# A layer norm, linear attention and gated MLP block on one core: the order of the first eleven microseconds

## The chip, the cores and the metric

The kernel runs on one core of a Trainium2 chip. The metric is the device time of one execution in microseconds (us); lower is better.

## The reference

One sequence of 2048 tokens with 448 features. The input is normalised once; a linear attention with 16 heads of 28 and an MLP with 1792 hidden units both read the normalised input, and the MLP's output gates the attention's. All inputs are bf16.

```python
x  = A_x                                   # (1, 2048, 448)
xn = (x - mean(x)) / sqrt(var(x) + 1e-5)   # over the 448 features

q, k, v = split(xn @ wqkv)                 # (448, 3*448), 16 heads of 28
phi = lambda t: where(t > 0, t + 1, exp(t)) + 1e-6
kv  = einsum("bhsd,bhse->bhde", phi(k), v)
z   = einsum("bhsd->bhd", phi(k))
o   = einsum(phi(q), kv) / (einsum(phi(q), z) + 1e-6)
s   = o @ wo

h = relu(xn @ w1 + b1) ** 2                # (448, 1792)
g = silu(h @ w2 + b2)                      # (1792, 448)
out = x + s * g
```

## The kernel before

**Tiles.** The 2048 tokens are 16 tiles of 128, in four groups of four. The 448 features are contracted in three full chunks of 128 rows and a rest of 64. In `xn` the last 64 columns are copied once more beside themselves (the "twin", L529), so that a transposed rest fills 128 rows and two matmuls with 64 rows each can stand side by side in the array. The 1792 hidden units are 14 blocks of 128; `H g.f` is block f of token group g.

**Who orders the work.** The function builds a list of operations with `add`, each with an engine, an estimated duration, what it reads and writes, and in some cases other engines that could take it (`alts`). `schedule` then plays the list through a model in time. TensorE ("pe") and SP keep the order in which the code names their operations. ScalarE ("act"), VectorE ("dve") and GpSimd ("pool") are planned greedily: among the operations that are ready, the one with the smallest due time `late` goes first, and `prio` sets that due time by hand. Transfers are modelled with one shared stream that is free from `dma_free` on (L118). The plan fixes each engine's order, the engine of operations with alternatives, and the PSUM bank of each buffer. `emit` writes the order out with semaphore waits; on the chip each engine then runs its list in that order, and a waiting instruction holds everything behind it on its engine.

**Transfers of the head.** SP issues them one after another: x tile 0, x tile 1, x tiles 2 and 3 in one transfer (`load_x`, L450 to L452), the first 384 rows of w_k (`load_main`, L453), then w1 in three blocks of columns, with the boundaries in `cuts` (L449: 512, 768 and 512 columns), each as 384 rows and two rests of 32 to 96 KB each (`load_rest`); b1 goes behind the first block, x tiles 4 to 7 behind the second. The two rests of w_k and the first rest of the first w1 block are issued from ScalarE. A matmul of block f waits for all transfers of the w1 block in which it lies (L770); blocks 0 and 1 (`HA = 2`) are the "head" blocks and are treated apart.

**The first group, tiles 0 to 3.** Per tile (L1211): `bn` and `ag` are statistics on VectorE (L483, L484), `ln` and `rs` give the reciprocal deviation on ScalarE (L491, L495), `xn` is the norm on VectorE (L513). `pe_transpose` turns the three full chunks on TensorE (L590) and copies them out of PSUM on ScalarE or VectorE (L600, L599): in its call `((0, 3, "act"),)` names chunks 0 to 3 and the engine of the copy. `pe_transpose_rests` does the rest chunk of two tiles (L614, copy on ScalarE L624). `k_part` are k's matmuls for one tile (L788), `k_rests` the 64-row rest of two tiles (L803), followed by the feature map phi (exp on ScalarE, two steps on VectorE). `head_part(lo, fi)` are the full chunks of w1 block fi for tiles lo and lo+1 (L816), `head_rest` their 64-row rest for all four tiles (L832). `warm(n)` emits n matmuls on a tile of zeros, whose result nobody reads (L1206); `warm(9, [("mv", 0)])` also waits for the statistics of tile 0. `bias_cols` turns b1 into columns (L1221).

TensorE runs this in the order in which it stands from L1226 on. Behind it come, at L1331, blocks 2 to 13 of group 0 in pairs (L773): first the pair of blocks 2 and 3, then, eight matmuls later, blocks 4 and 5, and so on. The rest of the kernel (q, k, the MLP's second matmul L1079, the attention's sums, the gate) follows on TensorE in a fixed order as well.

Of the kernel before, what the change touches and what calls it, by code (L numbers as in the profile page):

```python
# [9 lines left out]
P = 128  # L10
S, D, F = 2048, 448, 1792
# [35 lines left out]
class Program:  # L47
# [5 lines left out]

    def add(self, eng, emit, reads=(), writes=(), dur=0.2, alts=(), nbytes=0, mode=None, label="", slow=1.0):
        op = Op(eng, emit, reads, writes, dur, alts, nbytes, mode, label)
        op.slow = slow
        for t in op.reads:
            op.raw.add(self.writer[t])
            self.readers.setdefault(t, []).append(op)
        for t in op.writes:  # L60
            w = self.writer.get(t)
            if w is not None and w is not op:
                op.deps.add(w)
            for r in self.readers.get(t, ()):
                if r is not op:
                    op.deps.add(r)
            self.writer[t] = op
            self.readers[t] = [r for r in self.readers.get(t, ()) if r is op]
        op.raw.discard(op)
        op.deps |= op.raw  # L70
        for d in op.deps:
            d.succ.append(op)
        self.ops.append(op)
        return op
# [23 lines left out]
    def one_pass(self):  # L98
# [16 lines left out]
                        users[b].append(op)  # L115
        bank_last = [None] * PSUM_BANKS
        free = dict.fromkeys(self.ENGINES, 0.8)
        dma_free = 2.3  # L118
        last_mode = None
        order = {e: [] for e in self.ENGINES}  # L120
        pend = {e: [] for e in self.ENGINES}
# [4 lines left out]

        def ready(op):
            r = 0.0
            for d in op.deps:
                if d.end is None:  # L130
                    return None
                same = d.eng == op.eng == "pe" and d is not op.sync
                r = max(r, d.end + (0.0 if same else 0.05 if d.nbytes else LAT[d.eng]))
            return r
# [14 lines left out]
        while n:  # L149
            best = None  # L150
            for e in self.ENGINES:
                if e in fixed:
                    if not pend[e]:
                        continue
                    op = pend[e][0]
                    r = ready(op)
                    if r is None:
                        continue
                    new = [b for b in op.writes if isinstance(b, Buf) and b.bank is None]
                    banks = []  # L160
                    if new:
# [4 lines left out]
                        r = max(r, times[len(new) - 1][0])  # L166
                    st = max(r, free[e] + (SWITCH if e == "pe" and last_mode not in (None, op.mode) else 0.0))
                    cand = (st, 0, op, e, banks, op.dur)
                else:
# [13 lines left out]
                    for op in pend[e]:  # L183
                        r = ready(op)
                        if r is not None:
                            cands.append((max(r, free[e]), op))
                    for o in floating:
                        if o.end is None:
                            for ae, _ in o.alts:
                                if ae == e and o.eng != e:  # L190
                                    r = ready(o)
# [3 lines left out]
                    for st, op in cands:  # L195
                        if op.alts:
                            mine = op.dur if op.eng == e else dict(op.alts)[e]
                            others = [(op.eng, op.dur)] + list(op.alts)
                            r = ready(op)
# [7 lines left out]
                    if not keep:  # L207
                        continue
                    m = min(keep, key=lambda k: k[0])
                    st, op, du = min(  # L210
                        (k for k in keep if k[0] <= m[0] + min(0.6 * m[2], 0.02 + max(0.0, 0.3 * (m[1].late - k[1].late)))),
                        key=lambda k: k[1].late,
                    )
# [3 lines left out]
            st, _, op, e, banks, du = best  # L217
# [8 lines left out]
            if op.nbytes:  # L226
                free[e] = st + op.dur
                s2 = max(dma_free, st + 1.0)
                dma_free = s2 + op.nbytes * op.slow / (280e3 if s2 < 13.0 else 330e3)
# [76 lines left out]
def bass_recurrent_scan__linear_attn_block__dense_activation_squared_relu__prompt_kernel(  # L306
    nc, A_x, A_wqkv, A_wo, B_x, B_w1, B_b1, B_w2, B_b2, out
):
    with ExitStack() as es:
        sb = lambda name, shape, dtype: es.enter_context(nc.sbuf_tensor(name, shape, dtype))  # L310
        bf, f32 = dt.bfloat16, dt.float32
        pr = Program()
# [14 lines left out]
        w_k = sb("w_k", [P, 4, D], bf)  # L327
# [10 lines left out]
        mv = sb("mv", [P, NT, 2], f32)  # L338
# [79 lines left out]
        def tiles(t, lo, hi):  # L418
            if hi <= 2:
                return t[0][P * lo : P * hi].rearrange("(p s) d -> p s d", s=1)  # L420
            base, n = (2, 2) if hi <= 4 else (lo // 4 * 4, 4)
            v = t[0][P * base : P * (base + n)].rearrange("(p s) d -> p s d", s=n)
            return v[:, lo - base : hi - base, :]

        def dma(eng, dst, src, writes, nbytes, reads=(), dur=0.45, slow=1.0):
            return add(
                eng, lambda e, _: e.dma_start(dst, src), reads, writes, dur, nbytes=nbytes, label="dma" + str(writes[0]), slow=slow
            )

        def load_x(lo, hi, eng="sp"):  # L430
            dma(eng, x_tok[:, lo:hi, :], tiles(A_x, lo, hi), [("x", i) for i in range(lo, hi)], (hi - lo) * P * D * 2)

        def load_main(eng, w, src, name, lo, hi, c0=0, c1=3, off=0):
            dma(
                eng, w[:, c0:c1, lo:hi],
                src[128 * c0 : 128 * c1, off + lo : off + hi].rearrange("(c p) j -> p c j", p=P),
                [(name, c) for c in range(c0, c1)], 128 * (c1 - c0) * (hi - lo) * 2,
            )

        def load_rest(eng, w, src, name, lo, hi, off=0):  # L440
            for i in (0, 1):
                dma(
                    eng if isinstance(eng, str) else eng[i], w[64 * i : 64 * i + 64, 3, lo:hi], src[384:448, off + lo : off + hi], [(name, 3 + i)],
                    64 * (hi - lo) * 2, dur=0.58,
                )

        wn = lambda name: [(name, i) for i in range(5)]
        HA = 2
        cuts = (0, 4 * P, 10 * P, F)  # L449
        load_x(0, 1)  # L450
        load_x(1, 2)
        load_x(2, 4)  # L452
        load_main("sp", w_k, A_wqkv, "wk", 0, D, off=D)  # L453
        load_rest("act", w_k, A_wqkv, "wk", 0, D, off=D)
        for n, (lo, hi) in enumerate(zip(cuts, cuts[1:])):
            load_main("sp", w_1, B_w1, f"w1{n}", lo, hi)
# [125 lines left out]
        def pe_transpose(si, pieces):  # L582
            for lo, hi, eng in pieces:
                b = Buf("T")

                def f(e, _, lo=lo, hi=hi, b=b):
                    v = ps(b)[:, :].bitcast(bf)
                    last = None
                    for c in range(lo, hi):
                        last = e.transpose(v[:, (c - lo) * P : (c - lo + 1) * P], xn[:, si, c * P : (c + 1) * P], ident[:, :])  # L590
                    return last

                add("pe", f, [("xn", si), "ident"], [b], 0.0558 * (hi - lo), mode="128", label=f"T{si}.{lo}")

                def ev(e, eng, lo=lo, hi=hi, b=b):
                    src = ps(b)[:, 0 : 64 * (hi - lo)].bitcast(bf)
                    dst = xT[:, si, lo:hi, :].rearrange("p c k -> p (c k)")
                    if eng == "dve":
                        return e.tensor_copy(dst, src)  # L599
                    return e.activation(out=dst, in_=src, func=AF.Copy)  # L600

                n = hi - lo
                add(
                    eng, ev, [b], [("xT", si, c) for c in range(lo, hi)],
                    0.15 + 0.07 * n if eng == "dve" else 0.18 + 0.107 * n, label=f"eT{si}.{lo}",
                ).prio = -30
# [178 lines left out]
        def k_part(si, lo, hi):  # L785
            def f(e, _):
                for c in range(lo, hi):
                    last = e.matmul(  # L788
                        ps(k_head[si])[:, 0:D], xT[:, si, c, :], w_k[:, c, :], start=(c == 0), stop=False, skip_group_check=True
                    )  # L790
                return last

            add(
                "pe", f, [("wk", c) for c in range(lo, hi)] + [("xT", si, c) for c in range(lo, hi)] + ([k_head[si]] if lo else []),
                [k_head[si]], (hi - lo) * MM(D), mode="128", label=f"K{si}.{lo}",
            )
# [30 lines left out]
        def head_rest(lo):  # L827
            fs = (lo, lo + 1)

            def f(e, _):  # L830
                for h, fi in enumerate(fs):
                    last = e.matmul(  # L832
                        ps(head[fi])[:, 0:512], w_1[half[h], 3, fi * P : (fi + 1) * P], xT[half[h], 0:4, 3, :], start=False,
                        stop=True, skip_group_check=True,
                    )
                return last

            bs = [head[fi] for fi in fs]
            add("pe", f, [("xT", i) for i in range(4)] + [("w10", 3), ("w10", 4)] + bs, bs, MM(512), mode="64", label=f"Hr{lo}")
            for fi in fs:  # L840
                h_out(head[fi], 0, fi)
# [358 lines left out]
        def warm(n, after=()):  # L1200
            b = Buf("W")

            def f(e, _):
                last = None
                for _i in range(n):
                    last = e.matmul(ps(b)[:, 0:P], dum[:, 0:P], dum[:, 0:P], start=True, stop=True)  # L1206
                return last

            add("pe", f, ["dum", *after], [b], n * 0.075, mode="128", label="warm")
# [13 lines left out]
            )  # L1223
            add("act", lambda e, _: e.activation(out=b1f[:, :], in_=ps(bb)[:, 0 : NF // 2].bitcast(bf), func=AF.Copy), [bb], ["b1f"], 0.2, label="b1f")

        warm(31)  # L1226
        warm(9, [("mv", 0)])
        pe_transpose(0, ((0, 3, "act"),))
        warm(7)
        pe_transpose(1, ((0, 3, "dve"),))  # L1230
        k_part(0, 0, 3)
        pe_transpose_rests(0)
        k_part(1, 0, 3)
        head_part(0, 0)
        pe_transpose(2, ((0, 3, "dve"),))
        head_part(0, 1)
        k_rests(0)
        warm(4)
        pe_transpose(3, ((0, 3, "dve"),))
        bias_cols()  # L1240
        pe_transpose_rests(2)
        warm(4)
        head_part(2, 0)
        head_part(2, 1)
        head_rest(0)

        def ln(lo, hi):
            for si in range(lo, hi):
# [91 lines left out]
        a, b = "G10|G11", "G12|G13"  # L1340
# [37 lines left out]
```

## Time and profile before

| | |
|---|---|
| runs | 144.44, 144.80, 144.85 us; median 144.8 |
| the profiled execution | 144.75 us; span from first to last instruction 143.0 us |
| granted TensorE clock | 1.00 |
| TensorE matmul busy | 139.0 us (97% of the span), 1310 matmuls |
| VectorE busy | 104.3 us (73%) |
| ScalarE busy | 77.2 us (54%) |
| GpSimd busy | 6.4 us (4%) |
| chain that ended last | 96% on TensorE |
| HBM read, written | 9.23 MB, 1.90 MB |

TensorE counts as busy with any matmul, the fillers of L1206 among them. "L773" is line 773 of the kernel; a row of the timeline gives the start, the time from the first start to the last end of the merged instructions, the engine, the operation, what it writes and reads, and in brackets how long the engine was idle before and what ended that. A row of the chain gives the start, how long the chain ran through this engine and line, and how many instructions that were. A row of transfers gives the issuing queue, how many, KB of each and the median us from issue to landing. Starts and lengths are in us.

### The profile page before, as it was taken

To read this page: it belongs to the slowest core of one execution; us is meant where nothing else is said; L and a number is where in the kernel's file an instruction comes from. 1 tells how busy PE (TensorE), PEld (TensorE's weight loads), DVE (VectorE), ACT (ScalarE), POOL (GpSimd) and SP (SyncE) were. 2 spreads that over 40 slices of the span, in tenths; PEclk is the share of its full clock that TensorE was granted. 3 is DMA by queue.
4 is the path that set the end of the run, shared out by engine and by line. 5 is a ranking of instruction groups with operands and counts; after the bars stand their busy time and mean duration, and the time that the engine had idled before them with its cause. 6 is when DMAs were issued, how large, how long until landed. Compare 5 with 4: busy or idle time off the path is not lost.

```text
span 143.0 us, 3268 instructions
## 1 busy us (share of the span) xinstructions
PE 139.0 (97%) x1310; PEld 72.2 (50%) x1310; DVE 104.3 (73%) x226; ACT 77.2 (54%) x142; POOL 6.4 (4%) x40
## 2 busy tenths in 40 slices
PE   7999999999999999999999999999999999999991
PEld 7964445554444444444544444435546455555471
DVE  2779998997398899769787799782035727865874
ACT  3566996030788724997862787698139430202311
POOL 7900000000000000000000000000000000000000
PEclk9999999999999999999999999999999999999999
DMA  4999995259732000223000000000687001223032
GB/s 110 305 300 306 322 306 91 38 141 291 86 49 37 5 0 0 46 43 54 9 5 0 0 0 5 0 0 18 171 197 152 3 5 34 94 64 101 32 126 67
DMA packets 23500, 12.91 MB, mean 90 GB/s; under 512 B 14274, under 2 KB 22718, under 8 KB 23486
## 3 DMA queue, kind: packets, MB, share of 16 engines
q1 hardware_dynamic: 21758, 11.40, 31.2%
q10 hardware_dynamic: 1728, 1.31, 4.2%
q8 instruction: 10, 0.16, 0.5%
q14 instruction: 4, 0.03, 0.1%
HBM read 9.23 MB, written 1.90 MB: 78 GB/s over the span
## 4 chain that ended last, share of the span: by engine, by line
PE 96%; DVE 2%; issue 0%
PE pb L773 29%; PE pb L1079 22%; PE pb L1171 7%; PE pb L874 7%; PE pb L716 6%; PE pb L726 6%; PE pb L1206 4%; PE pb L1096 4%; PE pb L1136 3%; PE pb L853 1%; DVE gbuf L1160 1%; PE pb L880 1%; PE pb L816 1%; PE pb L1023 1%; PE pb L788 1%; PE pb L590 1%
## 5 line engine op out<-in xcount | busy, mean ns | idle before, releaser
L773 PE MATMUL pb<-xT,w 64*128 64x512 bf16 x378 | 43.6, 376 | 0.0
L1079 PE MATMUL pb<-w,r 64*128 64x448 bf16 x336 | 34.1, 349 | 0.0
L751 ACT ACTIVATE r<-pb,b1f 128x512 bf16<-128x512 f32 x40 | 25.9, 687 | 14.2 <-PE pb L773 13.4
L773 PEld LDWEIGHTS pb<-xT,w 64*128 64x128 bf16 x378 | 18.4, 94 | 21.7
L1079 PEld LDWEIGHTS pb<-w,r 64*128 64x128 bf16 x336 | 16.3, 94 | 15.8 <-issue 0.4
L748 DVE TENSOR_SCALAR r<-pb,b1f 128x512 bf16<-128x512 f32 x16 | 11.7, 748 | 5.5 <-PE pb L773 5.3
L763 ACT ACTIVATE r<-r 128x1024 bf16<-128x1024 bf16 x14 | 14.6, 1061 | 0.5 <-DVE r L748 0.4
L1191 DVE TENSOR_TENSOR gbuf<-pb,gbuf 128x448 bf16<-128x448 f32 x14 | 8.1, 619 | 6.1 <-PE pb L1171 6.1
L483 DVE BATCH_NORM_STATS2 st<-x_tok 128x6 f32<-128x448 bf16 x16 | 9.4, 616 | 3.1 <-DMA x_tok<-in_A_x_dram 2.9
L716 PE MATMUL pb<-w_k,xT 64*128 64x448 bf16 x98 | 11.6, 349 | 0.0
L1069 DVE TENSOR_TENSOR gbuf<-pb,b2b 128x448 bf16<-128x448 f32 x14 | 8.1, 617 | 4.1 <-PE pb L1079 2.2
L726 PE MATMUL pb<-xT,w_q 64*128 64x512 bf16 x84 | 11.0, 376 | 0.0
L1119 ACT ACTIVATE gbuf<-gbuf 128x448 bf16<-128x448 bf16 x14 | 7.0, 570 | 6.8 <-DVE gbuf L1069 5.9
L1171 PE MATMUL pb<-w_k,pqT 64*128 64x448 bf16 x96 | 10.6, 349 | 0.0
L987 DVE TENSOR_TENSOR pqT<-pqT,xT 128x2048 bf16<-128x2048 bf16 x3 | 3.7, 1218 | 8.8 <-DMA xT<-scr 8.8
L874 PE MATMUL pb<-pk,xn 128*128 128x448 bf16 x48 | 9.6, 353 | 0.0
L694 ACT ACTIVATE pk<-pb 128x448 bf16<-128x448 f32 x16 | 7.8, 545 | 3.1 <-PE pb L716 2.5
L706 DVE SCALAR_TENSOR_TENSOR pk<-pb,pk 128x448 bf16<-128x448 f32 x16 | 9.3, 617 | 0.0
L762 DVE TENSOR_TENSOR r<-r 128x1024 bf16<-128x1024 bf16 x14 | 9.1, 683 | 0.1
L694 ACT ACTIVATE pqT<-pb 128x512 bf16<-128x512 f32 x12 | 6.5, 597 | 3.3 <-PE pb L726 3.3
L910 DVE TENSOR_TENSOR zacc<-zacc,pk 128x448 f32<-128x448 f32 x13 | 8.1, 620 | 0.2
L706 DVE SCALAR_TENSOR_TENSOR pqT<-pb,pqT 128x512 bf16<-128x512 f32 x12 | 7.8, 683 | 0.1
(98 smaller groups left out, 135.3 us busy)
## 6 DMA issues: line engine op xcount, KB each, us to landing
out_dram<-gbuf SPq DMA_DIRECT2D x15, 112.0 KB, 1.7
w<-in_B_w_dram SPq DMA_DIRECT2D x1, 1568.0 KB, 10.5
x_tok<-in_A_x_dram SPq DMA_DIRECT2D x3, 448.0 KB, 6.0
xT<-gbuf SPq DMA_DIRECT2D x32, 32.0 KB, 2.0
w<-in_B_w_dram SPq DMA_DIRECT2D x2, 384.0 KB, 6.0
xT<-scr SPq DMA_DIRECT2D x6, 112.0 KB
w<-in_B_w_dram SPq DMA_DIRECT2D x1, 576.0 KB, 5.8
xT<-scr ACTq DMA_DIRECT2D x5, 112.0 KB
```

The costliest lines, as they stand in the source:

```text
L483: add("dve", lambda e, _: e.bn_stats(st6[:, si, :], x_tok[:, si, :]), [("x", si)], [("st", si)], 0.61, label=f"bn{si}").prio = hp(si, 0)
L694: "act", lambda e, _: e.activation(out=slot, in_=ps(buf)[0:rows, 0:n], func=AF.Exp), [buf, "actw"],
L706: lambda e, _: e.scalar_tensor_tensor(out=slot, in0=ps(buf)[0:rows, 0:n], scalar=1.0 + 1e-6, in1=slot, op0=ALU.add, op1=ALU.max),
L716: return e.matmul(ps(b)[:, 0:D], x_tile(rows, si, c), w_k[rows, c, :], start=start, stop=stop)
L726: return e.matmul(ps(b)[:, 0:512], w_q[rows, c, m * P : (m + 1) * P], x_group(rows, g, c), start=start, stop=stop,)
L748: return e.tensor_scalar(out=slot, in0=ps(b)[:, 0:512], scalar1=b1f[:, fi : fi + 1], scalar2=0.0, op0=ALU.add, op1=ALU.max)
L751: return e.activation(out=slot, in_=ps(b)[:, 0:512], func=AF.Relu, bias=b1f[:, fi : fi + 1])
L763: return e.activation(out=both, in_=both, func=AF.Square)
L773: return e.matmul(ps(b)[:, 0:512], w_1[rows, c, fi * P : (fi + 1) * P], x_group(rows, g, c), start=start, stop=stop,)
L874: last = e.matmul(ps(b)[:, 0:D], xn_cols(si, c * P, (c + 1) * P), pk[:, si, :], start=(si == 0), stop=(si == NT - 1),)
L1079: return e.matmul(ps(b)[:, 0:D], r_cols(rows, fi, si), w_2[rows, fi, :], start=start, stop=stop)
L1171: return e.matmul(ps(b)[:, 0:D], w, msb[rows, c, :], start=start, stop=stop)
```

## The change

All edits concern the head or its plan: VectorE's order for tiles 0 to 3 is written out by hand (a new field `behind`, which lets an operation be planned only after another has ended); w_k is loaded ahead of x tiles 2 and 3; the first w1 block shrinks from 512 to 256 columns, the second grows from 768 to 1024; the copies of the transposes of tiles 1 and 2 move from VectorE to ScalarE; 55 fillers become 43 in other places; and the planner's stream of transfers is taken to be free 0.3 us sooner in its model. The planner plans the whole kernel anew with these. The words of the change also name fewer constants; the diff has no such edit.

```diff
     def add(self, eng, emit, reads=(), writes=(), dur=0.2, alts=(), nbytes=0, mode=None, label="", slow=1.0):
         op = Op(eng, emit, reads, writes, dur, alts, nbytes, mode, label)
-        op.slow = slow
+        op.slow, op.behind = slow, None
...
-        dma_free = 2.3
+        dma_free = 2.0
...
         def ready(op):
             r = 0.0
+            if op.behind is not None:
+                if op.behind.end is None:
+                    return None
+                r = op.behind.end
...
-        cuts = (0, 4 * P, 10 * P, F)
+        cuts = (0, 2 * P, 10 * P, F)
         load_x(0, 1)
         load_x(1, 2)
+        load_main("sp", w_k, A_wqkv, "wk", 0, D, off=D)
         load_x(2, 4)
-        load_main("sp", w_k, A_wqkv, "wk", 0, D, off=D)
         load_rest("act", w_k, A_wqkv, "wk", 0, D, off=D)
...
-        warm(31)
-        warm(9, [("mv", 0)])
+        warm(28)
+        warm(5, [("mv", 0)])
         pe_transpose(0, ((0, 3, "act"),))
-        warm(7)
-        pe_transpose(1, ((0, 3, "dve"),))
+        warm(5)
+        pe_transpose(1, ((0, 3, "act"),))
         k_part(0, 0, 3)
         pe_transpose_rests(0)
         k_part(1, 0, 3)
         head_part(0, 0)
-        pe_transpose(2, ((0, 3, "dve"),))
+        pe_transpose(2, ((0, 3, "act"),))
         head_part(0, 1)
         k_rests(0)
-        warm(4)
         pe_transpose(3, ((0, 3, "dve"),))
         bias_cols()
         pe_transpose_rests(2)
-        warm(4)
+        warm(5)
         head_part(2, 0)
         head_part(2, 1)
         head_rest(0)
+
+        order = "bn0 ag0 bn1 ag1 xn0 xn1 bn2 ag2 bn3 ag3 xn2 xn3".split()
+        byname = {op.label: op for op in pr.ops}
+        for a, b in zip(order, order[1:]):
+            byname[b].behind = byname[a]
+            byname[b].prio = -25 + order.index(b)
```

## The prediction

> **What bounds the kernel now.** I read the chain of waits first, in order of time. It lies on TensorE from 1.06 us to 138.86 us, so what counts is whether that engine does work or only filler.
>
> ```profile
> 6.96 0.65 PE pb L788 x3
> 7.61 0.11 PE pb L614 x2
> 7.72 0.57 PE pb L788 x3
> 8.29 0.33 PE pb L816 x3
> 8.62 0.17 PE pb L590 x3
> 8.78 0.33 PE pb L816 x3
> 9.11 0.29 PE pb L803 x2
> 9.41 0.33 PE pb L1206 x4
> 9.74 0.17 PE pb L590 x3
> ...
> 10.46 0.73 PE pb L816 x6
> 11.19 0.32 PE pb L832 x2
> 11.51 9.06 PE pb L773 x84
> ```
>
> L1206 is the filler ("warm"). From L773 on the matmuls are back to back: the view of waits has no TensorE row from 11 us to the end. A gain in the head is therefore a shift of the first L773, by the timeline at 11.35 us, and everything behind it moves along. Next I read the timeline of the head, to see what sets that start.
>
> ```profile
> 5.46 0.63 DVE L483 BATCH_NORM_STATS2 st<-x_tok 128x6 f32<-128x448 bf16 x1 [0.44 <-DMA x_tok<-in_A_x_dram]
> 6.00 0.40 DVE L513 TENSOR_SCALAR xn<-x_tok,mv,rstd 128x448 bf16<-128x448 bf16 x1
> ...
> 7.28 0.62 DVE L483 BATCH_NORM_STATS2 st<-x_tok 128x6 f32<-128x448 bf16 x1
> ...
> 9.10 0.39 DVE L513 TENSOR_SCALAR xn<-x_tok,mv,rstd 128x448 bf16<-128x448 bf16 x1
> ...
> 9.94 0.36 DVE L599 COPY xT<-pb 128x384 bf16<-128x384 bf16 x1 [0.23 <-PE pb L590]
> ```
>
> VectorE waits for x tiles 2 and 3 until 5.46, takes statistics 2 ahead of norm 1, and so norm 3 runs at 9.10 and the last copy of a transpose (eT3) ends at 10.30. The partial w1 matmuls of tiles 2 and 3 (L816) follow at 10.36, their rest (L832) at 11.12, L773 at 11.35. Last I read the transfers, issue by issue, with us to landing.
>
> ```profile
> x_tok<-in_A_x_dram SPq DMA_DIRECT2D x1, 224.0 KB, 3.7
> w_k<-in_A_wqkv_dram SPq DMA_DIRECT2D x1, 336.0 KB, 4.4
> w<-in_B_w_dram SPq DMA_DIRECT2D x1, 576.0 KB, 5.8
> w<-in_B_w_dram SPq DMA_DIRECT2D x1, 96.0 KB, 5.6
> ```
>
> With their issues (1.71, 2.23, 4.85, 5.81 us): x2-3 lands at 5.44, w_k at 6.61, the second w1 block at 10.69, its last rest at 11.45. That block is first read by the second pair of column blocks, eight matmuls into L773 at 12.2, so it has 0.75 us in hand.
>
> **The change, part by part.**
>
> *Norm 1 ahead of statistics 2.* rstd 1 is ready at 5.27, so norm 1 runs at 5.30 instead of 6.00, for nothing: VectorE waited for x2-3 there.
>
> *Copies 1 and 2 on ScalarE.* Copy 0, same shape on ScalarE, took 0.49; the VectorE copies took 0.36. So +0.13 each in latency, and 0.72 us taken off VectorE. Copy 1: transpose 1 can issue at 5.94, after copy 0's transpose (norm 0 ends 5.01, so 5.08 to 5.40) and five fillers of 0.107; it is done at 6.47, the copy 6.50 to 6.99. ScalarE is idle there. Copy 2 is priced below; it falls between rstd 3 and the first exp, and nothing queued behind it is held.
>
> *w_k ahead of x2-3 on SP's queue.* Two issues swap (0.60 and 0.48 us); no other queue is passed and no issue is added, ScalarE's and POOL's queues stay as they are. w_k now starts 0.52 earlier and without 224 KB in front: between 5.44 (if it goes as x2-3 went) and 6.09 (6.61 less the issue). K0, after transpose 1, wants it at 6.26: no wait at either end. x2-3 now ends where w_k ended, 6.61, since the same bytes lie in front. It may be earlier: the 16 DMA engines moved 250 GB/s in 4.5 to 5.0 us against 336 in 5 to 6, while w_k's packets were only beginning (the first at 4.54); the larger transfer in third place fills that, (336-250)*0.5 = 43 KB, or 0.13 us at 336. Bounds 6.3 to 6.61; I take 6.46, close to the filled case. This edit costs x2-3 1.0 us, and the order of VectorE must pay for it:
>
> - statistics 2 at 6.46, its aggregate 7.11 (0.65 later, as 2.89 to 3.55), statistics 3 at 7.20, aggregate 7.86, norm 2 at 7.95 to 8.33 (8.19 before: 0.14 late), ln and exp 3 at 8.07 to 8.59 (0.52 from aggregate end, as before), norm 3 at 8.62 to 9.01 (9.49 before). Before, statistics 3 waited from 6.73 to 7.28 behind a copy and its transpose; that stall is gone.
> - TensorE: K0 6.26, the two tails 7.0, K1 (copy 1 at 7.06), first w1 part to 8.0. All covered by transpose 2, which waits for norm 2: 8.40. Then by the chain's rows: transposes 0.17, w1 part 0.33, K tails 0.29 plus a switch of 0.09: transpose 3 at 9.29 against 9.575. Its condition, norm 3 at 9.01, is met.
> - Copy 2 runs 8.78 to 9.27. Copy 3 then runs 9.66 to 10.02 against 10.30. Second w1 parts at 10.08; fillers (five at 0.056 after the tails of 2 and 3) end at 10.05, just in time.
> - The tails' copy on ScalarE (0.39) comes either straight behind the first exp (ends about 10.4) or behind both (10.85). L832 wants it at 10.84: 0 or 0.07. I take 0, as it had priority at 10.31 before only once both exps had run, and keep 0.07 for the range.
>
> So by this path L773 starts at 11.35 - 0.28 = **11.07**.
>
> *Fewer fillers.* 55 become 43. Nine of the twelve ran at 0.107 ahead of transpose 1 and held transpose 0 from about 5.08 to 5.20; that 0.1 is in the sum. The four ahead of transpose 3 go: without that, 0.22 of the 0.28 would be lost.
>
> *First w1 block 256 instead of 512 columns.* 192 KB of main part less ahead of the first w1 part, which waited for it 0.23 us until 8.07: it now lands some 0.65 us sooner (192 KB at 300 GB/s), about 7.3, and the wait is gone, but the wait for norm 2 at 8.40 covers it, so it is worth nothing by itself. Its price: column blocks 2 and 3, the **first** pair of L773, now lie in the second block. What had 0.75 us in hand is now asked for at once, and the pair waits for all three of its transfers. Behind that wait in TensorE's queue lies everything. The bytes up to its last rest are the same. Landing: 11.45 as before, or earlier by the 0.13 above, and by packet sizes: the packet records have medians 41, 46, 69 ns for 896, 1024, 1536 bytes, some 8 ns plus 0.037 a byte, so 512 packets of 512 and 512 of 2048 take an estimated 56.6 us of engine time against 58.9, 0.14 us over 16 engines. I estimate 11.18; bounds 10.9 and 11.9, because the last of 16 engines came 0.5 behind the fifteenth in that transfer (10.92 and 11.45) and can be anywhere. A matmul follows about 0.1 behind a landing (8.04, 8.13): **11.27**.
>
> The later of 11.07 and 11.27 decides. The sum: 11.27 - 11.35 = -0.08, say -0.1.
>
> *Planner's constant and the stated order.* No instruction is added; the plan may give other engines to relus and squares. TensorE waits nowhere after 11 us, and w_2 lands at 22.2 for a need at 23.06; I price it at 0, bounds -0.1 (a tail of VectorE and ScalarE after TensorE's last matmul, little to win) and +0.3 (one relu late, half its 0.69).
>
> [...] Between the fillers' end (33*0.107 after 1.06, 4.6) and transpose 0 at 5.08, TensorE is idle for half a microsecond, where it was never idle before. In the trace filler matmuls stood 0.107 us apart until 6.26, and L788 dropped from 0.31 to 0.19 between its first and second matmul, at 7.07: TensorE was at half rate for 6 us. [...] The rival below prices it from rows.
>
> **Rivals.**
> 1. *The second w1 block comes as late as before or later* (0.2): 11.45 + 0.1 = 11.55, +0.2, 144.95 us. For: same bytes, and the slow engine. Against: better packets. It decides from a landing of 11.25 on; with 0.4 us more of skew, 145.3.
> 2. *The second block is off the path* (0.2): it lands by 10.95, and the compute path's 11.07 holds: -0.28, 144.47; with x2-3 at 6.3 and the block at 10.8, -0.45.
> 3. *Half rate goes on past 8 us* (0.1): slower. K0 from 6.26 at twice its rows is 1.12, tails 0.22, K1 1.12, w1 part 0.65: 9.37 instead of 8.0, so transpose 2 is late by 1.0; to 10.3 the next parts cost double as well, another 0.3 to 0.4. Together +1.1 after what was won: 145.9. It decides once K0 to the first w1 part take more than 2.1 us. For: the new idle gap. [...]
> 4. *It doesn't do what it says*: "fewer constants" removes no instruction of POOL in the diff, and a plan with other orders costs TensorE a wait (0.05): +0.5, 145.25.
>
> **How the numbers follow.** The profiled execution took 144.75 us with a span of 143.0; the runs' median is 144.8 (144.44 to 144.85). 144.75 - 0.1 = 144.65. My forecast, the two gates nearly level, has 0.45. A tenth lies below 144.1 (rival 2 at its best, other shifts) and a tenth above 145.5 (rival 3, rival 1 with skew): range 144.1 to 145.5; the likeliest case alone 144.4 to 144.9. Faster or slower counts from 0.3%, 0.43 us, about what a measurement of this kernel can tell from no change: below 144.37 or above 145.23. Faster: half of rival 2 and a fifth of the forecast, 0.2. Slower: rivals 3 and 4, a third of rival 1 and a little of the forecast, 0.26. Within: 0.54.
>
> **What would show it.** Norm 1 at about 5.3, statistics 2 at 6.4 to 6.6, norm 3 by 9.1, L773 starting within 0.2 us of 11.27 with a wait on a w1 transfer ahead of it. Wrong if L773 starts below 11.0 (x2-3 and the block earlier than the queue's bytes say), if K1's matmuls are 0.37 apart, or if TensorE waits after 12 us.

## The result and the profile after

The changed kernel takes 145.94 us (median of 18 runs) against 144.66 for the kernel before in the same runs; the ratio is 1.0064, 95% interval 1.0041 to 1.0086. Medians and ranges in this document are over all runs, while a ratio compares the means of the fast ones, here 145.60 us over 16 (148.1 and 146.67 count as slow) with 144.68, so it is not the ratio of the medians. The forecast was 144.65, with a range of 144.1 to 145.5. The kernel is slower, and it scatters: its runs lie between 144.43 and 146.67 us but for one at 148.1, those of the kernel before between 144.44 and 144.90.

The profiled execution took 145.42 us with a span of 143.6, so 0.67 more than the one before. The page's chain of waits now names a transfer, which the one before did not:

```profile
PE 89%; DMA 4%; SPq 3%; DVE 1%; issue 0%
```

In order of time the head's part of that chain is short (start, length, what):

```profile
5.27 0.50 SPq L431
5.77 0.04 issue
5.81 6.00 DMA w<-in_B_w_dram
11.81 0.05 issue
11.86 9.24 PE pb L777 x84
```

All lines are 4 to 9 higher than before; L777 is the old L773, L836 the old L832. The last rest of the second w1 block is issued at 5.81, lands at 11.81, and L777 starts at 11.86. In the profile before, L773 starts 0.51 earlier, although L832 ahead of it starts 0.27 later than L836 does now:

```profile
11.12 0.39 PE L832 MATMUL pb<-xT,w 64*128 64x512 bf16 x2
...
11.35 9.23 PE L773 MATMUL pb<-xT,w 64*128 64x512 bf16 x84
```

The view of waits after the change gives TensorE one row from 11 us to the end:

```profile
PE pb L777 <- DMA w<-in_B_w_dram: 0.6, 1, 0.6
```

The timeline shows the path ahead of it:

```profile
4.85 0.50 PE L594 MATMUL pb<-ident,xn 128*128 128x128 bf16 x3
...
5.11 0.40 DVE L517 TENSOR_SCALAR xn<-x_tok,mv,rstd 128x448 bf16<-128x448 bf16 x1 [0.32 <-ACT rstd L499]
...
6.00 0.76 PE L792 MATMUL pb<-w_k,xT 128*128 128x448 bf16 x3
...
6.49 0.63 DVE L487 BATCH_NORM_STATS2 st<-x_tok 128x6 f32<-128x448 bf16 x1 [0.98 <-DMA x_tok<-in_A_x_dram]
...
8.65 0.40 DVE L517 TENSOR_SCALAR xn<-x_tok,mv,rstd 128x448 bf16<-128x448 bf16 x1 [0.32 <-ACT rstd L499]
...
9.67 0.36 DVE L603 COPY xT<-pb 128x384 bf16<-128x384 bf16 x1 [0.39 <-PE pb L594]
...
10.08 0.83 PE L820 MATMUL pb<-xT,w 128*128 128x256 bf16 x6
...
10.85 0.39 PE L836 MATMUL pb<-xT,w 64*128 64x512 bf16 x2
...
11.86 9.24 PE L777 MATMUL pb<-xT,w 64*128 64x512 bf16 x84 [0.62 <-DMA w<-in_B_w_dram]
```

Norm 1 at 5.11, statistics 2 at 6.49, norm 3 at 8.65, copy 3 until 10.03, L836 at 10.85: the head is done 0.27 sooner than before (11.12), and L777 could have started at 11.07, 0.22 behind L836 (0.23 before). The transfers of this execution, each with KB and us to landing:

```profile
w_k<-in_A_wqkv_dram SPq DMA_DIRECT2D x1, 336.0 KB, 4.0
x_tok<-in_A_x_dram SPq DMA_DIRECT2D x1, 224.0 KB, 4.2
w<-in_B_w_dram SPq DMA_DIRECT2D x1, 768.0 KB, 6.0
w<-in_B_w_dram SPq DMA_DIRECT2D x1, 128.0 KB, 6.0
```

With their issues (1.72, 2.24, 4.83, 5.81): w_k lands at 5.76, x2-3 at 6.46, the second block's main part at 10.80 and its last rest at 11.81.

### The profile page after: what moved, and what is told of

Its sections match the earlier page's. It is cut to its first block, busy times and chain, and to the rows that moved or that the text cites. A ratio compares the mean times of both kernels' runs of the same rounds, so it can differ in the third digit from the quotient of the medians.

```text
span 143.6 us, 3241 instructions
## 1 busy us (share of the span) xinstructions
PE 138.3 (96%) x1298; PEld 71.0 (49%) x1298; DVE 103.2 (72%) x222; ACT 78.9 (55%) x146; POOL 6.2 (4%) x40
## 4 chain that ended last, share of the span: by engine, by line
PE 89%; DMA 4%; SPq 3%; DVE 1%; issue 0%
PE pb L777 29%; PE pb L1083 22%; PE pb L1175 7%; PE pb L878 6%; PE pb L720 6%; PE pb L730 6%; DMA w<-in_B_w_dram 4%; PE pb L1100 4%; SPq L431 3%; PE pb L1140 3%; PE pb L857 1%; DVE gbuf L1164 1%; PE pb L884 1%; PE pb L1027 1%; PE pb L952 1%; PE pb L1053 1%
## 5 line engine op out<-in xcount | busy, mean ns | idle before, releaser
L777 PE MATMUL pb<-xT,w 64*128 64x512 bf16 x378 | 43.6, 376 | 0.6 <-DMA w<-in_B_w_dram 0.6
L755 ACT ACTIVATE r<-pb,b1f 128x512 bf16<-128x512 f32 x41 | 26.5, 687 | 14.9 <-PE pb L777 14.4
L777 PEld LDWEIGHTS pb<-xT,w 64*128 64x128 bf16 x378 | 18.3, 94 | 22.5 <-DMA w<-in_B_w_dram 0.9
L752 DVE TENSOR_SCALAR r<-pb,b1f 128x512 bf16<-128x512 f32 x15 | 11.0, 748 | 6.2 <-PE pb L777 6.0
## 6 DMA issues: line engine op xcount, KB each, us to landing
w<-in_B_w_dram SPq DMA_DIRECT2D x1, 1568.0 KB, 10.9
```

The source lines that it names most:

```text
L752: return e.tensor_scalar(out=slot, in0=ps(b)[:, 0:512], scalar1=b1f[:, fi : fi + 1], scalar2=0.0, op0=ALU.add, op1=ALU.max)
L755: return e.activation(out=slot, in_=ps(b)[:, 0:512], func=AF.Relu, bias=b1f[:, fi : fi + 1])
L777: return e.matmul(ps(b)[:, 0:512], w_1[rows, c, fi * P : (fi + 1) * P], x_group(rows, g, c), start=start, stop=stop,)
```

## The experiments

Two ways to read the loss stood against each other from the start. **Block theory**: the first pair of column blocks waits for the second w1 block. **Rate theory**: TensorE stays at half rate (in the profiles fillers start 0.107 us apart early in the head and 0.056 later) behind the new idle gap. A third, the **queue theory**, held that the swap delays all transfers. Each ratio is to the kernel before, run in turn on the same chip.

### 512 columns first again

```diff
-        cuts = (0, 2 * P, 10 * P, F)
+        cuts = (0, 4 * P, 10 * P, F)
```

> The changed kernel with the first w1 block at 512 columns again. Block theory (L777 waits for the second w1 block, whose last rest landed at 11.81 us): the first pair of column blocks reads the first block, which lands by 8.1, L777 starts at 11.07, 0.8 earlier than in the changed kernel; about 144.4 us, at or 0.25 below the kernel before, and the scatter of the changed kernel (144.4 to 148.1) is gone. Rate theory (the idle gap ahead of the first transpose leaves TensorE at half rate in some runs): the scatter stays and the median stays near 145.9. Queue theory (the swap of w_k and x2-3 delays all transfers): L777 waits for something else and the time stays above 145.2.

Median 144.95 us over 12 runs (144.46 to 145.58), ratio 1.0013 (0.9996 to 1.0030). The wait on w1 ahead of L777 and the runs near 146 are gone, so the block theory holds. But the 0.25 did not come. In the profiled execution x1 landed at 4.39 instead of 3.65 and x2-3 at 7.08 instead of 6.46:

```profile
7.10 0.63 DVE L487 BATCH_NORM_STATS2 st<-x_tok 128x6 f32<-128x448 bf16 x1 [0.74 <-DMA x_tok<-in_A_x_dram]
...
9.01 0.17 PEld L594 LDWEIGHTS pb<-ident,xn 128*128 128x128 bf16 x3 [0.26 <-DVE xn L517]
...
11.69 1.67 PE L777 MATMUL pb<-xT,w 64*128 64x512 bf16 x14
```

VectorE waits for x2-3 until 7.10, transpose 2 (9.01) waits for norm 2, and L777 starts at 11.69, 4.61 behind the landing; in the changed kernel's profile 6.46 and 11.07 stand 4.61 apart as well. With the swap, x2-3 sets the start. The chain view of this execution goes by the first w1 block instead (landed at 8.48); the 0.26 that TensorE waited for norm 2 speaks against that.

### 256 columns first, and nothing else changed

```diff
 # the kernel before
-        cuts = (0, 4 * P, 10 * P, F)
+        cuts = (0, 2 * P, 10 * P, F)
```

> The kernel before with the first w1 block at 256 columns and nothing else. Block theory: L773 waits for the second block's last rest, start at 11.5 to 12.2, 145.0 to 146.0 us with a scatter of 1 us or more from run to run. Rate theory: no new gap, so 144.7 with the old scatter of 0.4 us. Queue theory: the transfers stand in their old order, so 144.7 to 144.9.

145.68 us (144.75 to 146.89), ratio 1.0055 (1.0028 to 1.0081). One number reproduces the loss and the scatter, with the old transfers' order, the old fillers and no new gap.

```profile
PE pb L773 <- DMA w<-in_B_w_dram: 0.8, 1, 0.8
```

The last rest landed at 12.69, L773 started at 12.74. This speaks against the queue theory too.

### Four blocks of w1

```diff
-        cuts = (0, 2 * P, 10 * P, F)
+        cuts = (0, 2 * P, 4 * P, 10 * P, F)
...
-            if n == 1:
+            if n == 2:
                 load_x(4, 8)
```

> The changed kernel with w1 in four blocks of 256, 256, 768 and 512 columns: three issues more on SP, x tiles 4 to 7 still behind the block that ends at column 1280. Block theory: the first pair reads the second block, landed by 9; L777 starts at 11.07, 144.4 us, unless the added issues (1.6 us on SP) make the third block late for the second pair at 11.9; then up to 145.2. Rate and queue theories: 145.5 to 146.

145.06 us (144.65 to 145.46), ratio 1.0015 (0.9994 to 1.0036). The wait is gone as with 512 columns; in the profile x2-3 landed at 6.71 and L777 started at 11.32, again 4.61 behind. The expected 144.4 was missed for that reason.

### b1 issued from ScalarE

```diff
-                dma("sp", b1r[:, :], B_b1.rearrange("(f p) -> f p", p=P), ["b1r"], F * 2)
+                dma("act", b1r[:, :], B_b1.rearrange("(f p) -> f p", p=P), ["b1r"], F * 2)
```

> The changed kernel with b1's transfer issued from ScalarE, so that the second w1 block is issued 0.6 us sooner on SP. In the changed kernel the engines moved 147 GB/s between 6.5 and 7.0 us, before the block's packets flowed. Hole theory: the block lands 0.2 to 0.35 us sooner, and the time falls by as much, to about 145.6. If the block's lateness comes from its slowest engines alone: no difference, 145.9.

146.07 us (144.58 to 148.21; 145.74 over the seven runs in the ratio), ratio 1.0061 (1.0034 to 1.0087): no difference from the changed kernel. The block was issued 0.8 sooner (4.02 instead of 4.83), yet its last rest landed at 12.12 in the profile. The edit also moves the first rest of the first w1 block on ScalarE's queue, from 2.10 to 4.30; it landed at 11.14 and L836 ran at 11.23, but L777 (12.16) still waited for the second block. The earlier issue by SP did not help.

### Both edits of transfers undone

```diff
-        cuts = (0, 2 * P, 10 * P, F)
+        cuts = (0, 4 * P, 10 * P, F)
...
-        load_main("sp", w_k, A_wqkv, "wk", 0, D, off=D)
         load_x(2, 4)
+        load_main("sp", w_k, A_wqkv, "wk", 0, D, off=D)
```

> The changed kernel with both edits of transfers undone: first w1 block of 512 columns, x2-3 ahead of w_k. What is left are VectorE's order, the copies on ScalarE and the fillers. Landing theory: with the swap, L777 starts 4.61 us behind x2-3's landing (7.08 to 11.69 with 512 columns, 6.71 to 11.32 with four blocks), so the late and scattered landing of x2-3 ate what the order won; here x2-3 lands near 5.4, K0 waits for w_k at 6.65, the first w1 part for its block at 8.05, L777 at 11.1: 144.4 us, 0.25 to 0.4 below the kernel before, with its scatter. Rival (order, copies and fillers win nothing, whatever lands when): L777 at 11.3 to 11.4, 144.7.

144.73 us (144.51 to 145.04, and two at 146.93 and 146.95 that are not in the ratio) against 145.06 for the kernel before in the same runs, ratio 0.9978 (0.9953 to 1.0002). The profile has K0 behind w_k's landing (6.72), the first w1 part behind its block (8.11) and L777 at 11.16, as expected. The interval still touches 1.

### Four blocks, x2-3 ahead of w_k

The edits of the four blocks and the order of loads just above, together.

> Four w1 blocks (256, 256, 768, 512 columns) and x2-3 ahead of w_k, the rest as changed. Landing theory: the first w1 part no longer waits for 512 columns, so L777 comes 0.1 to 0.2 earlier than with three blocks, near 10.95: 144.2 to 144.4 us, unless the third block (one rest landed at 12.03) is late for the second pair at 11.8. Rival: 144.7 to 145.1 as with four blocks and w_k first.

145.23 us, ratio 1.0011 (0.9986 to 1.0035); L777 at 11.27 in the profile, because K0 waited for w_k until 7.0. The first w1 part no longer waited for its block, but that had cost nothing.

### The second block in rows of 1024 bytes

```diff
-            load_main("sp", w_1, B_w1, f"w1{n}", lo, hi)
+            if n == 1:
+                load_main("sp", w_1, B_w1, "w11", lo, 6 * P)
+                load_main("sp", w_1, B_w1, "w11b", 6 * P, hi)
+            else:
+                load_main("sp", w_1, B_w1, f"w1{n}", lo, hi)
...
-            names = wn("w1%d" % sum(fi * P >= c for c in cuts[1:]))
+            n = sum(fi * P >= c for c in cuts[1:])
+            names = wn("w1%d" % n) + ([("w11b", c) for c in range(3)] if n == 1 else [])
```

> The changed kernel, but the 384-row part of the second w1 block comes in two transfers of 512 columns, so in rows of 1024 bytes instead of 2048, with one issue more. The first pair still waits for all of it. If rows of 2048 bytes make the slowest engine late (last landing 1.5 to 2.0 us behind the median with them, 0.7 to 1.0 with 1536 bytes): the last rest lands by 11.4 and the time falls to 145.0 to 145.3. If single stalled packets hit any row size, or the added issue costs as much: 145.7 to 146.2 as before.

145.30 us (144.83 to 146.29), ratio 1.0015 (0.9987 to 1.0043), in the expected band for the row size. The last rest landed at 11.49, 1.06 behind the median of the 16 engines, and L777 (11.56) waited for x2-3's path (6.95), not for w1, if only by 0.07. The interval overlaps the changed kernel's by a hair, so the row size is likely, not settled.

### Old transfers, copies back on VectorE

```diff
 # on the run with both edits of transfers undone
-        pe_transpose(1, ((0, 3, "act"),))
+        pe_transpose(1, ((0, 3, "dve"),))
...
-        pe_transpose(2, ((0, 3, "act"),))
+        pe_transpose(2, ((0, 3, "dve"),))
```

> As the run with the old transfers, and the copies of transposes 1 and 2 back on VectorE. If the copies on ScalarE carry part of the win (VectorE free for statistics 3 and norm 2): L777 0.2 to 0.3 later, 144.6 to 144.8. If VectorE has room for them, because it waits for x2-3 or for rstd 3 anyway: the same within 0.1.

144.77 us, ratio 0.9976 (0.9953 to 1.0000). L777 started at 11.37 against 11.16 with the copies on ScalarE: the head loses the expected 0.2. Yet the times are the same; "Copies on ScalarE" below comes back to this.

### VectorE's order alone, and the swap alone

The order alone: the kernel before with `behind` and the list of names. The swap alone:

```diff
 # the kernel before
-        load_x(2, 4)
         load_main("sp", w_k, A_wqkv, "wk", 0, D, off=D)
+        load_x(2, 4)
```

> The kernel before with VectorE's stated order alone (norm 1 ahead of statistics 2); transfers, copies and fillers as before. If the order is what wins in the run with the old transfers (L777 at 11.16 against 11.35 before): K0 still waits for w_k at 6.65 and the fillers ahead of transpose 3 stay, so L773 at 11.2 to 11.35, ratio 0.998 to 1.000. If it needs the fewer fillers to show: ratio 1.000.

> The kernel before with w_k ahead of x2-3 and nothing else. Landing theory: statistics 2 wait for x2-3 until 6.5 to 7.1 and norm 1 stands behind them on VectorE, so transpose 1, K0 and all that follows come 0.4 to 1.0 later: L773 at 11.7 to 12.3, ratio 1.003 to 1.007. If the swap is harmless (w_k was what K0 waited for, and it comes sooner): ratio 1.000.

The order alone: 144.97 us, ratio 1.0013 (0.9990 to 1.0036), no win to be seen. In its profile one DMA engine brought w_k's last part at 7.48, a microsecond behind the other fifteen, and K0 waited 1.43 us for it: L777 at 12.14. The swap alone: 145.30 us, ratio 1.0026 (1.0012 to 1.0039). It costs, though less than expected, since the planner, told of the later x2-3, by itself put norm 1 ahead of statistics 2 (5.16 and 6.65 in the profile, where L773 starts at 11.45).

### w_k issued from ScalarE

```diff
 # on the run with both edits of transfers undone
-        load_main("sp", w_k, A_wqkv, "wk", 0, D, off=D)
+        load_main("act", w_k, A_wqkv, "wk", 0, D, off=D)
...
-            load_rest(("act", "sp") if n == 0 else "sp", w_1, B_w1, f"w1{n}", lo, hi)
+            load_rest("sp", w_1, B_w1, f"w1{n}", lo, hi)
```

> As the run with the old transfers (512 columns first, x2-3 third on SP), but the 384 rows of w_k issued first from ScalarE and both rests of the first w1 block from SP. Between 3.5 and 4.0 us the engines moved 142 GB/s in the kernel before; w_k's packets fill that, so w_k lands by 5.6 and the first w1 block by 7.5, while x0 and x1 may land 0.3 later. Landing theory: L777 at 10.4 to 10.8, 143.9 to 144.3 us, ratio 0.994 to 0.997. Rival: x0 and x1 share the engines with w_k from 2.2 us on, and the whole chain behind norm 0 moves back by what w_k gains: ratio 0.998 or more.

145.96 us (five runs from 144.60 to 145.12, seven from 145.89 to 146.73), ratio 1.0039 (1.0004 to 1.0074): the rival came true, and something more. w_k landed at 4.21, but x1 at 4.59 instead of 3.53, and TensorE stood idle for 1.11 us:

```profile
1.78 2.98 PE L1210 MATMUL pb<-dum 128*128 128x128 bf16 x26
...
5.87 0.50 PE L594 MATMUL pb<-ident,xn 128*128 128x128 bf16 x3 [1.11 <-DVE xn L517]
...
7.01 1.33 PE L792 MATMUL pb<-w_k,xT 128*128 128x448 bf16 x3
...
8.35 1.33 PE L792 MATMUL pb<-w_k,xT 128*128 128x448 bf16 x3
...
9.47 0.82 PE L820 MATMUL pb<-xT,w 128*128 128x256 bf16 x3
...
10.11 0.35 PE L594 MATMUL pb<-ident,xn 128*128 128x128 bf16 x3
```

Three K matmuls take 1.33 here and 0.73 at full rate (L788 at 7.56 in the kernel before). Half rate lasted until about 9.9, three microseconds longer than in the kernel before. It held this execution up: norm 3 was done by 9.01, but transpose 3, which reads it, came at 11.02 and L777 at 12.80. TensorE was busy again from 5.87, so the step came four microseconds after work resumed. The time from start of work to the step was not the same in every trace: in the run with 256 columns first and nothing else changed, the fillers began at 1.06 and stood 0.056 apart from 4.00 on, 2.9 us later; in the kernel before they began at 1.06 as well and the step came at 7.07, 6.0 us later. Nor did a long gap bring half rate each time: with 512 columns first again TensorE was idle for 0.94 us ahead of transpose 0 and ran that at full rate, at 5.60 (three matmuls in 0.34, against 0.50 here). That the gap of 1.11 us is the cause is therefore not shown. So the rate theory had to be tried on the changed kernel itself.

### The changed kernel without the gap, and the best version without it

```diff
-        warm(5, [("mv", 0)])
+        warm(10, [("mv", 0)])
```

once in the changed kernel, once in the version with old transfers and copies on VectorE.

> The changed kernel with 38 fillers instead of 33 ahead of transpose 0, so that TensorE has no idle time there (0.36 us in the changed kernel's profile, 0.94 and 1.11 in two other runs, in one of which half rate lasted until 9.9). L777 still waits for the second w1 block. Landing theory: median 145.6 to 146.2 and single runs from 144.4 to 147, as the changed kernel. Rate theory (part of the changed kernel's slow runs are runs at half rate): nothing above 145.5, median below 145.3.

> Old transfers, copies on VectorE, VectorE's stated order, the changed fillers behind transpose 0 and 38 fillers ahead of it: what the runs so far point to as the best. Landing theory: L777 at 11.0 to 11.3, ratio 0.996 to 0.999, and no runs above 145.5. If the idle time ahead of transpose 0 was harmless: the same as with 33 fillers, 0.9976.

The changed kernel with the gap closed: 145.26 us (144.68 to 146.82), ratio 1.0033 (1.0004 to 1.0062), between the two expectations; in its profile L777 waited 0.84 us and started at 12.17, 0.05 behind the last rest (12.12). The best version: 144.72 us (144.34 to 145.48), ratio 0.9995 (0.9982 to 1.0008). The last is no slower than the run without the five fillers (144.77, ratio 0.9976): the kernel before, beside which each is measured, took 144.79 here and 145.06 there. Nothing here beats the kernel before beyond its interval.

### Four more profiles of the changed kernel

No edit; single profiled executions.

> The changed kernel itself, one more profiled execution. Landing theory: L777 starts 0.05 us behind the last rest of the second w1 block, later than 11.07 by the whole time above 144.45, with TensorE at full rate by 7. Rate theory: in an execution of 145.9 or more L792's matmuls are 0.37 apart past 8 us and L777's wait for the block is short or absent.

> The changed kernel itself, a second look, with the same expectations as the first.

> The changed kernel itself, a third look, with the same expectations as the first.

> The changed kernel itself, a fourth look, with the same expectations as the first.

The table has them beside the first profile. "Median" and "last" are the landings of the second block's last rest on the middle and on the slowest of the 16 DMA engines, from the trace's semaphore updates; "ready" is L836's start plus 0.22.

| time | x2-3 lands | ready | block: median | block: last | L777 starts | time less start |
|---|---|---|---|---|---|---|
| 145.42 | 6.46 | 11.07 | 10.31 | 11.81 | 11.86 | 133.56 |
| 146.69 | 6.81 | 11.42 | 10.19 | 13.09 | 13.13 | 133.56 |
| 146.50 | 7.25 | 11.85 | 10.67 | 12.89 | 12.94 | 133.56 |
| 145.31 | 6.92 | 11.52 | 10.75 | 11.70 | 11.74 | 133.57 |
| 146.20 | 6.45 | 11.05 | 10.37 | 12.60 | 12.64 | 133.56 |

The view of waits of the first and the fourth of these, TensorE's only row in each:

```profile
PE pb L777 <- DMA w<-in_B_w_dram: 1.5, 1, 1.5
```

```profile
PE pb L777 <- DMA w<-in_B_w_dram: 1.4, 1, 1.4
```

The third has no such row: there L777 came only 0.22 behind "ready". In all five, L777 starts 0.04 to 0.05 behind the last engine's landing, and the time is that start plus 133.56. K1's matmuls took 0.73 for three and began by 7.4 in every one: no half rate past 8 us. What differs from run to run is how late the slowest DMA engines are. In the three executions above 146 us it was a single one, 1.55 to 1.90 behind the fifteenth; in the first profile the fifteenth was late as well (11.63).

## Why the prediction was wrong

**The compute path, 11.07: right to the hundredth in the profile.** Norm 1 without cost (5.11), x2-3 at 6.46 (predicted 6.46), norm 3 at 8.65 (8.62), copy 3 until 10.03 (10.02), ready at 11.07 (11.07). But that agreement is in part luck: x2-3 at 6.46 was among the best of these five executions (6.45 to 7.25), so the path was ready at 11.05 to 11.85, and the -0.28 is its good end. The "Bounds 6.3 to 6.61" held in only three of the eleven profiled executions with the swap (the latest 7.25); the swap's price was mis-sized by up to 0.8.

**The step that failed: "I estimate 11.18", with "bounds 10.9 and 11.9", for the second w1 block.** The mechanism, "the pair waits for all three of its transfers", was named, and so was its place on the path; rival 1 had it. The size was off: the last rest landed at 11.70 to 13.09 in the five executions. The bytes and packets were right enough: the median engine landed at 10.19 to 10.75, where 10.45 stood before. What was taken as a small skew is the term that decides: the last engine came 0.95 to 2.90 behind the median (1.00 before). Rival 1 was given 0.2 and at most 145.3; it was the outcome, at 145.94. By the table's last column the median run, which was not profiled, would have L777 at 145.94 - 133.56 = 12.38. The same edit alone has a ratio of 1.0055, and undoing it leaves 1.0013: that shows it. Why the slowest engine is so late is open.

**The packet estimate.** 512-byte packets took a median of 27 ns (27 from the line), 2048-byte ones 84 (84). In the profile before, the 1536-byte packets have a median of 74 over the whole block, not 69, which would put the block 0.29 earlier rather than 0.14; so the miss is not in the medians but in the stalls. In the changed kernel's profile single 2048-byte packets of the block took 1174 and 1066 ns, and 21 of the 512 in all took over 250; in the profile before one 1536-byte packet did (831).

**Half rate past 8 us (rival 3).** Not in any of the five executions; that its 145.9 is so near the measured median is luck. That the new gap speaks for it was the author's guess, which no run shows: in the first profile after the change the gap is there (matmul starts 0.41 us apart, the weight loads idle for 0.36), and L792 dropped from 0.22 to 0.19 between its first and second matmul, at 6.22, sooner than the step at 7.07 of the kernel before. In the run with w_k from ScalarE half rate did last past 8 us, behind an idle gap of 1.11 us, in one execution. That half rate lasted so long in some unprofiled run isn't excluded: with the gap closed the ratio was 1.0033, and its interval overlaps that of the changed kernel.

**Copies on ScalarE, "nothing queued behind it is held".** True inside the head (0.2 gained: 11.16 against 11.37), but a term was missing. In all 19 profiled executions of this study the last landing of an output stands 131.21 to 131.23 behind the first L773 or L777, so the planner's new order behind the head was worth 0 within the span, as priced. The time outside the span, however, is 1.72 to 1.75 in the six executions with these two copies on VectorE and 1.85 to 1.90 in the thirteen with them on ScalarE. So about 0.15 us that no view of the span shows goes with the engine of these copies; of the profiled execution's 0.67, 0.51 is L777's later start and 0.15 this. With the copies the planner moved one relu more to ScalarE (41 instead of 40) in twelve of the thirteen, but where ScalarE had only 39 of them (b1 from ScalarE) the time outside was 1.87 as well. What it is was not tried.

**Fewer fillers, 256 columns for the first part.** The first w1 part's own wait went as said (its block landed at 7.09, it ran at 7.36 behind K1), and it was worth nothing, as said.

## What to carry to other kernels

Before splitting a transfer to get its first part sooner, look at who reads the second part first and how much time that reader had in hand: here 0.75 us of slack were traded for a wait that cost nothing. Here the wait on a transfer ended with the slowest of its 16 engines (L777 started 0.04 to 0.05 behind that landing in all five executions), so give such a wait a range from the spread of landings, not a landing from bytes; the median engine landed ahead of the path in all five executions (10.75 at the latest, against 11.05 at the earliest), and L777 waited in all five. And compare the time outside the span too when a kernel's instructions move between engines: it differed by about 0.15 us here.

## What the runs showed that was not expected

- In some executions one of the 16 DMA engines was a microsecond or more behind the rest (1.55 to 1.90 behind the fifteenth in the three above 146 us). In the fourth further profile the lateness stayed through the transfers that followed: the last landing is 1.9 to 2.2 behind the fifteenth for each of the second block's three transfers and for x tiles 4 to 7. For the last rest of the w1 block that ends at column 1280 the slowest engine was 0.95 to 2.90 behind the median in the eight executions whose block came in rows of 2048 bytes (four of them above 1.9), and 0.29 to 1.72 in the ten with rows of 1536 (six of them below 0.95). The run with rows of 1024 for the main part had 1.06 and no wait. Why an engine was so late stays open.
- The step to full rate came anywhere between about 4.0 and 7.1 us in these traces, and at about 9.9 behind the gap of 1.11 us, while the profile's granted clock read 1.00 there; here the rate could be read only from the matmuls' distance (fillers 0.107 against 0.056 us, three K matmuls in 1.33 against 0.73).
- The time outside the span moved by about 0.15 us with two copies' engine (1.72 to 1.75 with VectorE, 1.85 to 1.90 with ScalarE).
